# K projections ahead of Q, x of tiles three and four second in SyncE's queue, all MLP weights issued from ScalarE's queue, and new written-out orders, in a one-core transformer block

## The chip, the cores and the metric

The kernel runs on one core of one Trainium2 chip. The metric is the time of one execution on the device in microseconds (us). Three runs of the kernel before took 193.61, 193.75 and 194.16 us: median 193.75 us.

## The reference

What is computed is one transformer block on x of 2048 tokens by 448 channels, in bfloat16: linear attention with 16 heads of 28 channels, then a gated MLP with 1792 hidden channels, each behind a layer norm and with a residual.

```python
def _A_ref(x, wqkv, wo):
    qkv = (x @ wqkv).reshape(B, S, 3, H, Dh) -> 3, B, H, S, Dh
    phi = lambda t: jnp.where(t > 0, t + 1, jnp.exp(t)) + 1e-6
    pq, pk = phi(q), phi(k)
    kv = jnp.einsum("bhsd,bhse->bhde", pk, v)
    z = jnp.einsum("bhsd->bhd", pk)
    num = jnp.einsum("bhqd,bhde->bhqe", pq, kv)
    den = jnp.einsum("bhqd,bhd->bhq", pq, z)[..., None] + 1e-6
    return merge_heads(num / den) @ wo

def _B_ref(x, w_gate, w_up, w_down):
    return (_gelu(x @ w_gate) * (x @ w_up)) @ w_down

h  = x + _A_ref(_layernorm(x), wqkv, wo)
h2 = h + _B_ref(_layernorm(h), w_gate, w_up, w_down)
```

kv and z are sums over all tokens, so no attention output can be formed before the K side of every token is done.

## The kernel before

**Tiles and stages.** The 2048 tokens are 16 tiles of 128. Tensor names are those of the profile; the names in this list are those of the recorded work items, and t is the tile.

1. *Layer norm of x.* bnst1_t and bnag1_t (lines 413 and 414, VectorE) give mean and variance, ln1_t and rstd1_t (lines 420 and 422, ScalarE) the inverse deviation. Tiles 0 to 3 are normalised on VectorE (normD_t, line 435), transposed on TensorE (tr0_t and tr1_t, line 443: two halves), and copied out of PSUM by ScalarE (evxA_t, line 448) and VectorE (evxD_t, line 450). Tiles 4 to 15 are normalised on GpSimd (negm1_t and normP_t, lines 417 and 453) and transposed by a DMA transpose on SyncE's queue (xT_t, line 455).
2. *K side.* k_t is four matmuls of 448 columns (line 469), ek_t its exponential on ScalarE (line 480), ck_t and pk_t two VectorE steps that make phi(k) (lines 481 and 482). The V projection is folded: pt_t multiplies phi(k) by the normalised x itself (line 488; four matmuls for a tile up to tile 9, from tile 10 on split into pt1_t, whose column block also carries z, and pt3_t), summed over all tiles in four PSUM banks.
3. *Q side.* q_t is again four matmuls (line 469), then eq_t and rq_t on ScalarE (lines 496 and 497), and later cq_t, aq_t on VectorE (lines 564 and 565; for pairs p of tiles from the third pair on cqP_p, aqP_p in lines 582 and 583).
4. *The middle.* When the last pt has ended, the sums are copied out (evpD_3 line 516, z1 and z0 lines 514 and 515, evpA_0, evpA_1, evpD_2 lines 519 and 521), multiplied with the V weights (kv, line 527), masked (kvm, line 531), multiplied with the output weights (w2_c, line 547) and copied out again (evwA_c, evwD_c, lines 551 and 553). Two small DMAs (dws0, dws1, line 555) make a copy of these weights with its halves swapped.
5. *Attention output by pairs of tiles (a2_pair).* t1 multiplies by z (line 569 or 585), dr or drP sums (lines 572 and 586), de and rd make 1/den, pn or pnP (lines 576 and 590) normalises. Pair 0 is transposed on TensorE (tro, line 599), pairs 1 to 7 by a DMA transpose on SyncE's queue (oT_p, line 605). The output matmuls are out1_t (line 617) for pair 0 and outA_p, outB_p (lines 627 and 628: two matmuls run at once on the two halves of the rows) for the others. hr_t (line 633) adds the residual, bnst2_t and bnag2_t are the second layer norm's statistics; pair 0 is normalised on VectorE (nhD, wr64, lines 645 and 647) and transposed on TensorE (trh_0, trh_1, line 654; copied out by evhA_0 on ScalarE, line 658, and evhD_1 on VectorE, line 660), the other pairs on GpSimd (negm2, vpe2, pow2, nhP_t, lines 417, 425, 426, 662), copied by VectorE (wrap_t, line 664) and transposed by a DMA on SyncE's queue (hT_t, line 665).
6. *MLP.* In chunks of 2, 2, 4, 4 and 4 tiles. gu2_v or gu4_v (lines 726 and 728) is one unit of gate and up matmuls, which run at once on the two halves of the rows. Unit v writes PSUM bank v % 2 for gate and 6 + v % 2 for up; ge0_v, ge1_v (line 746, ScalarE) apply gelu and hm0_v, hm1_v (line 748, VectorE) multiply into the hidden tensor hh, which frees the banks for unit v + 2. gu2 units 0 to 6 are tiles 0 and 1, 7 to 13 tiles 2 and 3; gu4 units 14 to 27 are tiles 4 to 7, 28 to 41 tiles 8 to 11, 42 to 55 tiles 12 to 15. downA_p and downB_p (line 696) and, for the last two tiles, down448 and down224 (line 678) are the down projection, fo (lines 682, 702) the last residual, do_t (lines 683, 703) the store, on SyncE's queue.

**What sets the order.** Nothing is scheduled at run time. Every work item is recorded with an index; the table ORDERS (lines 15 to 49) has, for each of TensorE, ScalarE, VectorE, GpSimd and SyncE, the indices in the order in which the engine runs them. Semaphore waits are derived from what each item reads and writes. An engine takes its items strictly in order, so an item that waits holds up everything behind it on its engine. HOLD only picks which of several waits is put first. SEQ (line 246) sets the order in which projections are recorded, and with it the indices and which of four PSUM banks each projection gets in turn.

**The loads.** A DMA is issued from SyncE's or ScalarE's queue, in the order of that queue. SyncE's queue has x of tile 0, Wq, x of tiles 2 and 3, Wk, x of tiles 4 to 7, 8 to 11, 12 to 15, the V and output weights, then the twelve xT, then the four gate and up loads, then dws0, dws1, oT_1, oT_2, the down weights, and the later transposes and stores. ScalarE's queue has x of tile 1 and the last 64 rows of Wq and of Wk, then the table load.

The orders of the engines around the places that the prediction's steps touch, in names:

```
TensorE  ... k_12 k_14 pt3_10 k_15 pt1_11 pt1_12 pt1_13 pt3_11 pt3_12 pt1_14 pt1_15 pt3_13 pt3_14 pt3_15 q_4 q_5 kv ...
TensorE  ... out1_0 q_11 out1_1 q_10 q_13 q_15 q_14 outA_1 trh_0 trh_1 q_12 outB_1 gu2_0 gu2_1 outA_2 gu2_2 gu2_3 outB_2 ...
SyncE    ... hT_14 do_3 hT_15 do_4 hT_12 hT_13 ...
```

Of the kernel before, what the change touches and what calls it, by code (L numbers as in the profile page):

```python
# [48 lines left out]
)  # L49
HOLD = {  # L50
    32: (31,), 35: (34,), 66: (36,), 102: (101,), 127: (126,), 166: (165,), 188: (187,), 214: (213,), 294: (292,),
    305: (302,), 323: (302,), 362: (360,), 388: (387,), 498: (378,), 631: (630,), 707: (704,), 745: (744,), 786:
    (672,), 837: (836,), 864: (863,),
}


class _Buf:
# [172 lines left out]
def bass_sequential_preLN__linear_attn_block__glu_gated_geglu__prompt_kernel(  # L230
    nc, A_x, A_wqkv, A_wo, B_x, B_w_gate, B_w_up, B_w_down, out
):
    S, D, FF, H, DH = 2048, 448, 1792, 16, 28
# [14 lines left out]
    G = _Graph()  # L248
    es = ExitStack()
    with es:  # L250
# [8 lines left out]
        wqk_sb = sb("wqk_sb", [128, 4, 2 * D], BF16)  # L259
# [558 lines left out]
```

## Time and profile before

| | us |
|---|---|
| median of three runs | 193.75 |
| the profiled execution, its own time | 193.84 |
| its span (first to last instruction) | 191.9 |
| TensorE busy | 185.7 (97%) |
| VectorE busy | 128.4 (67%) |
| ScalarE busy | 75.2 (39%) |
| GpSimd busy | 50.7 (26%) |

TensorE's busy time is a union of pipelined matmuls, and successive matmuls overlap in it: a group of four matmuls of 448 columns is shown as 0.92 us long, but the next group starts 0.76 us later. So idle time of TensorE is read from starts: the start of one group to the start of the next, less the work of the first.

### The profile page before, as it was taken

Reading aid. Unit: us, or ns where it says so; the run is one execution under the profiler, and the core shown is the slowest. Engines: PE = TensorE matmul, PEld = TensorE weight load, DVE = VectorE, ACT = ScalarE, POOL = GpSimd, SP = SyncE. Lnnn points to the kernel's source line nnn. Section 1 sums busy time; section 2 is a strip of 40 time slices with the busy share of each in tenths; the row PEclk is TensorE's granted clock in tenths of the full one; section 3 lists DMA queues with packets and bytes.
Section 4 is the critical chain, followed back from the end, with each engine's and each line's share of the span. In section 5 each row is a group of like instructions: output and inputs, shape, how many; then the busy total and the mean of one; then the engine's idle time right before and its main releaser. Section 6 shows DMA issues by size and latency. Waiting matters only on the chain.

```text
span 191.9 us, 4456 instructions
## 1 busy us (share of the span) xinstructions
PE 185.7 (97%) x1813; PEld 107.3 (56%) x1813; DVE 128.4 (67%) x328; ACT 75.2 (39%) x220; POOL 50.7 (26%) x91
## 2 busy tenths in 40 slices
PE   7899999999899999999999999999998999999994
PEld 7454445655488677886455445444553445455454
DVE  3799879899799998899993863544723244415223
ACT  3689534699954222335132132432320233411200
POOL 6066730525503478235028000006300000000000
DMA  6985647999295505930221520000193000000025
GB/s 171 377 214 76 106 84 168 222 218 192 55 267 135 96 3 101 149 66 3 48 48 35 108 54 0 0 3 2 35 143 67 3 0 0 27 0 24 3 90 173
DMA packets 35077, 17.11 MB, mean 89 GB/s; under 512 B 26865, under 2 KB 33649, under 8 KB 35057
## 3 DMA queue, kind: packets, MB, share of 16 engines
q1 hardware_dynamic: 34752, 16.60, 40.9%
q8 instruction: 14, 0.23, 0.6%
q10 hardware_dynamic: 304, 0.23, 0.4%
q14 instruction: 7, 0.05, 0.1%
HBM read 8.26 MB, written 1.84 MB: 53 GB/s over the span
## 4 chain that ended last, share of the span: by engine, by line
PE 79%; DVE 11%; DMA 4%; ACT 3%; POOL 0%; SPq 0%; issue 0%
PE ps L728 38%; PE ps L696 19%; PE ps L726 7%; PE ps L469 4%; PE ps L488 3%; PE ps L678 3%; PE ps L627 3%; DMA x_sb<-in_A_x_dram 2%; DVE st L413 2%; PE ps L628 2%; DMA xnT<-xnn 2%; DVE pqn L576 1%; DVE den L572 1%; ACT e L480 1%; DVE x_sb L633 1%; DVE w L553 1%
## 5 line engine op out<-in xcount | busy, mean ns | idle before, releaser
L726 PE MATMUL ps<-hnT,wgu_sb 64*128 64x512 bf16 (+1 forms) x490 | 88.8, 333 | 0.7 <-DVE x_sb L702 0.7
L728 PE MATMUL ps<-hnT,wgu_sb 64*128 64x512 bf16 (+1 forms) x490 | 89.0, 333 | 0.0
L746 ACT ACTIVATE gl<-ps 128x256 bf16<-128x256 f32 x112 | 36.4, 383 | 81.8 <-PE ps L726 78.2
L748 DVE TENSOR_TENSOR hh<-ps,gl 128x256 bf16<-128x256 f32 x112 | 42.4, 416 | 38.6 <-ACT gl L746 38.4
L728 PEld LDWEIGHTS ps<-hnT,wgu_sb 64*128 64x128 bf16 x490 | 44.8, 94 | 31.2 <-DVE hh L748 4.6
L726 PEld LDWEIGHTS ps<-hnT,wgu_sb 64*128 64x128 bf16 x490 | 45.0, 94 | 6.3 <-DMA hnT<-hn 1.2
L696 PE MATMUL ps<-wd_sb,hh 64*128 64x448 bf16 x392 | 41.4, 349 | 0.0
L696 PEld LDWEIGHTS ps<-wd_sb,hh 64*128 64x128 bf16 x392 | 21.8, 94 | 15.8 <-issue 0.4
L469 PE MATMUL ps<-wqk_sb,xnT 128*128 128x448 bf16 x128 | 28.2, 355 | 1.0 <-DMA xnT<-xnn 0.4
L413 DVE BATCH_NORM_STATS2 st<-x_sb 128x6 f32<-128x448 bf16 x32 | 19.3, 615 | 3.2 <-DMA x_sb<-in_A_x_dram 3.1
L469 PEld LDWEIGHTS ps<-wqk_sb,xnT 128*128 128x128 bf16 x128 | 11.9, 98 | 12.7 <-DMA xnT<-xnn 1.3
L585 POOL TENSOR_TENSOR t<-pq,zbc 128x448 f32<-128x448 bf16 x12 | 13.0, 1104 | 19.6 <-DVE pq L583 18.1
L488 PE MATMUL ps<-pk,xnn 128*128 128x448 bf16 x64 | 13.9, 353 | 0.0
L627 PE MATMUL ps<-w,pqnT 64*128 64x448 bf16 x49 | 11.5, 349 | 0.8 <-DVE hn L647 0.8
L702 DVE TENSOR_TENSOR x_sb<-ps,x_sb 128x448 bf16<-128x448 f32 x14 | 8.4, 618 | 5.3 <-PE ps L696 5.3
L480 ACT ACTIVATE e<-ps 128x448 bf16<-128x448 f32 x16 | 8.6, 538 | 5.3 <-PE ps L469 5.1
L417 POOL TENSOR_SCALAR nm<-mv 128x1 f32<-128x1 f32 (+1 forms) x19 | 4.0, 218 | 24.3 <-DVE mv L414 24.0
L662 POOL TENSOR_SCALAR hn<-x_sb,nm,rs 128x448 bf16<-128x448 bf16 x14 | 10.3, 745 | 0.5
L628 PE MATMUL ps<-pt_sb,pqnT 64*128 64x448 bf16 x42 | 10.2, 350 | 0.0
L633 DVE TENSOR_TENSOR x_sb<-ps,x_sb 128x448 bf16<-128x448 f32 x16 | 9.7, 614 | 0.8 <-PE ps L628 0.8
L482 DVE SCALAR_TENSOR_TENSOR pk<-ps,e 128x448 bf16<-128x448 f32 x16 | 9.9, 619 | 0.2
L453 POOL TENSOR_SCALAR xnn<-x_sb,nm,rs 128x448 bf16<-128x448 bf16 x12 | 8.9, 743 | 3.5 <-ACT rs L422 2.9
(83 smaller groups left out, 155.5 us busy)
## 6 DMA issues: line engine op xcount, KB each, us to landing
out_dram<-x_sb SPq DMA_DIRECT2D x15, 112.0 KB, 1.8
wd_sb<-in_B_w_down_dram SPq DMA_DIRECT2D x1, 1568.0 KB, 8.0
x_sb<-in_A_x_dram SPq DMA_DIRECT2D x3, 448.0 KB, 6.3
wgu_sb<-in_B_w_gate_dram SPq DMA_DIRECT2D x1, 896.0 KB, 12.2
wgu_sb<-in_B_w_up_dram SPq DMA_DIRECT2D x1, 896.0 KB, 16.5
wqk_sb<-in_A_wqkv_dram SPq DMA_DIRECT2D x2, 336.0 KB, 4.4
wgu_sb<-in_B_w_gate_dram SPq DMA_DIRECT2D x1, 672.0 KB, 6.1
wgu_sb<-in_B_w_up_dram SPq DMA_DIRECT2D x1, 672.0 KB, 8.6
```

The source lines that it names most:

```text
L413: op("dve", lambda e: e.bn_stats(st[:, t, :], src_ap), [b_src], [b_st[t]], "bnst%s_%d" % (tag, t))
L469: ins = e.matmul(ps[:, bk, 0:D], xnT[:, t, k, :], wqk_sb[:, k, c0:c0 + D], start=(k == 0), stop=(k == 3))
L488: ins = e.matmul(ps[:, BK_PT[c], 0:D], xnn[:, t % XN_R, c * 128:(c + 1) * 128], pk[:, ip, :], start=(t == 0), stop=(t == T - 1))
L585: op("pool", lambda e, n=n: e.tensor_tensor(t1[:, n, :], pq[:, a + n, :], zbc[:, :], ALU.mult), [b_pq[a + n]] + b_z, [b_t1[n]], "t1p_%d" % ...
L627: e.matmul(ps[:, BK_OUT[0], 0:D], pqnT[ra, i2, sg // 2, :], w2[ra, sg // 2, :], start=(sg == 0), stop=(sg == 5))
L628: ins = e.matmul(ps[:, BK_OUT[1], 0:D], pqnT[rb, i2, 3 + (sg + 1) // 2, :], (w2 if sg == 6 else w2s)[rb, sg // 2, :], start=(sg == 0), sto ...
L633: op("dve", lambda e, t=t, bo=bo: e.tensor_tensor(x_sb[:, t, :], ps[:, bo, 0:D], x_sb[:, t, :], ALU.add), [b_ps[bo], b_x[t]], [b_x[t]], "h ...
L696: ins = e.matmul(ps[:, BK_O[n], 0:D], hh[rows, j, sl[n]], wd_sb[rows, j, :], start=(half == 0 and j == 0), stop=(half == 1 and j == NJ - 1))
L726: first = e.matmul(psG[:, jj * N:(jj + 1) * N], wgu_sb[A_, k, j * 128:(j + 1) * 128], hnT[A_, ka_, c0:c0 + N], start=(k == 0), stop=(k == ...
L728: ins = e.matmul(psU[:, jj * N:(jj + 1) * N], wgu_sb[B_, k, j * 128:(j + 1) * 128], hnT[B_, kb_, c0:c0 + N], start=(k == 0), stop=(k == NK ...
L746: G.add("act", lambda e, gi=gi, cs_=cs_, psG=psG: e.activation(gl[:, gi, cs_], psG[:, cs_], AF.Gelu_apprx_tanh), r=[b_ps[BK_G[i]]], w=[b_g ...
L748: op("dve", lambda e, dst=dst, srcU=srcU, srcL=srcL: e.tensor_tensor(dst, srcU, srcL, ALU.mult), [b_ps[BK_U[i]], b_glh], [b_ar[j_][t % HR] ...
```

## The change

The Wk loads take the place of the Wq loads at the head, on ScalarE's queue; x of tiles 2 and 3 moves up to second place in SyncE's queue. The four gate and up loads and the down-weight load move from SyncE's queue to ScalarE's. SEQ starts with K0 K1 in place of Q0, and all five orders are new.

```diff
-    SEQ = "Q0 K0 K1 Q1 K2 Q2 K3 K4 K5 Q3 K6 K7 ...
+    SEQ = "K0 K1 Q0 K2 K3 Q1 K4 Q2 K5 Q3 K6 K7 ...
...
         dma_x("sp", 0, 1)
         dma_x("act", 1, 2)
-        dma_w3("sp", wqk_sb, 0, D, b_wq, "dwq")
-        dma_w1("act", wqk_sb, 0, D, b_wq, "dwq_t")
         dma_x("sp", 2, 4)
-        dma_w3("sp", wqk_sb, D, 2 * D, b_wk, "dwk")
-        tx1 = dma_w1("act", wqk_sb, D, 2 * D, b_wk, "dwk_t")
+        dma_w3("act", wqk_sb, D, 2 * D, b_wk, "dw0")
+        dma_w1("act", wqk_sb, D, 2 * D, b_wk, "dw0_t")
+        tx1 = dma_w1("act", wqk_sb, 0, D, b_wq, "dw1_t")
+        dma_w3("sp", wqk_sb, 0, D, b_wq, "dw1")
...
-            dma("sp", wgu_sb[A_, :, cs], B_w_gate[:, cs]..., "dwg%d" % i, after=xts[-1:])
-            dma("sp", wgu_sb[B_, :, cs], B_w_up[:, cs]..., "dwu%d" % i, after=xts[-1:])
+            dma("act", wgu_sb[A_, :, cs], B_w_gate[:, cs]..., "dwg%d" % i, after=eks[11:12])
+            dma("act", wgu_sb[B_, :, cs], B_w_up[:, cs]..., "dwu%d" % i, after=eks[11:12])
...
-                dma("sp", wd_sb[:, :, :], B_w_down.rearrange("(j p) n -> p j n", p=128), [b_wd], "dwd", after=[G.all[-1]])
+                dma("act", wd_sb[:, :, :], B_w_down.rearrange("(j p) n -> p j n", p=128), [b_wd], "dwd")
```

`after=` only fixes an order on one queue; it is no wait. The two tables of indices say little in themselves. In names, the stretches of the new orders that matter here are:

```
TensorE  warm tr0_0 tr1_0 tr1_1 tr0_1 k_0 k_1 tr0_3 tr1_3 tr0_2 tr1_2 q_0 k_2 k_3 pt4_0 pt4_1 q_1 pt4_2 q_2 k_4 q_3 ...
         ... k_11 q_4 k_12 k_13 k_14 pt4_9 pt3_10 k_15 pt3_11 pt1_10 pt1_11 pt1_12 pt3_12 pt1_13 pt1_14 pt1_15 q_5 pt3_13 pt3_14 pt3_15 q_8 q_6 kv ...
         ... out1_0 out1_1 q_11 q_12 q_13 q_15 q_14 outA_1 trh_0 trh_1 outB_1 gu2_0 gu2_1 outA_2 gu2_2 outB_2 gu2_3 gu2_4 gu2_5 outA_3 gu2_6 outB_3 downA_0 ...
         ... gu4_33 downB_2 gu4_34 gu4_35 gu4_36 gu4_37 downA_3 gu4_38 gu4_39 downB_3 gu4_41 gu4_40 gu4_43 ...
VectorE  wqkpad bnst1_0 bnag1_0 bnst1_1 bnag1_1 normD_0 bnst1_3 normD_1 bnag1_3 evxD_0 bnst1_2 bnag1_2 evxD_1 normD_3 normD_2 ck_0 bnst1_4 ...
         ... pk_14 cq_1 ck_15 pk_15 cq_3 aq_2 aq_3 evpD_3 z0 aq_1 t1d_0 dr_0 evpD_2 ... wr64_0 wr64_1 pnP_2 aqP_3 evhD_1
         hr_2 hr_3 bnst2_2 drP_3 hm0_0 hm1_0 rdP_3 cqP_4 pnP_3 bnag2_2 hm1_1 hm0_1 bnst2_3 bnag2_3 hm0_2 hm1_2 hr_5 hr_4 hm1_3 hm0_3 ...
         ... bnst2_14 fo448_4 hm1_33 hm0_33 bnag2_14 hm1_34 hm0_34 hm0_35 hm1_35 fo448_5 wrap_14 hm1_37 hm1_36 wrap_13 wrap_15 hm0_36 wrap_12 ...
ScalarE  ... ek_13 dwg0 ek_14 dwu0 rq_4 ek_15 dwg1 eq_4 z1 eq_5 rq_5 dwu1 deA_0 evpA_1 evpA_0 ... tbl2 ge0_0 ge1_0 deP_3 dwd ge1_1 ...
SyncE    dx0 dx2 dw1 dx4 dx8 dx12 dwv dwv_t dwo xT_4 xT_5 xT_6 xT_7 xT_8 xT_10 xT_11 xT_9 xT_12 xT_13 xT_14 xT_15 dws0 dws1 oT_1 ...
         ... hT_8 do_3 do_4 do_0 hT_13 hT_15 hT_12 hT_14 do_2 ...
```

The work itself, the number and the shape of every matmul, VectorE, ScalarE and GpSimd instruction and of every transfer, is the same in both.

More of the change, by code (lines that the diff above doesn't have):

```diff
@@ L15 @@
 ORDERS = (
[33 rows of a table removed]
[34 rows of a table added]
 )
 HOLD = {
-    32: (31,), 35: (34,), 66: (36,), 102: (101,), 127: (126,), 166: (165,), 188: (187,), 214: (213,), 294: (292,),
-    305: (302,), 323: (302,), 362: (360,), 388: (387,), 498: (378,), 631: (630,), 707: (704,), 745: (744,), 786:
-    (672,), 837: (836,), 864: (863,),
+    32: (31,), 66: (36,), 99: (98,), 175: (174,), 188: (187,), 232: (231,), 294: (291,), 305: (298,), 362: (360,),
+    388: (387,), 498: (378,), 767: (764,), 787: (786,), 807: (806,), 839: (836,), 864: (863,),
 }
@@ L245, in bass_sequential_preLN__linear_attn_block__glu_gated_geglu__prompt_kernel @@
     T1_DVE = (0,)
-    SEQ = "Q0 K0 K1 Q1 K2 Q2 K3 K4 K5 Q3 K6 K7 K8 K9 K10 K11 K12 K13 Q4 K14 Q5 K15 Q6 Q7 Q8 Q9 Q10 Q11 Q12 Q13 Q14 Q15"
+    SEQ = "K0 K1 Q0 K2 K3 Q1 K4 Q2 K5 Q3 K6 K7 K8 K9 K10 K11 K12 K13 Q4 K14 Q5 K15 Q6 Q7 Q8 Q9 Q10 Q11 Q12 Q13 Q14 Q15"
     G = _Graph()
@@ L509, in bass_sequential_preLN__linear_attn_block__glu_gated_geglu__prompt_kernel @@
             cs = slice(0, FC) if i == 0 else slice(FC, FF)
-            dma("sp", wgu_sb[A_, :, cs], B_w_gate[:, cs].rearrange("(k p) n -> p k n", p=64), [b_wg[i]], "dwg%d" % i, after=xts[-1:])
-            dma("sp", wgu_sb[B_, :, cs], B_w_up[:, cs].rearrange("(k p) n -> p k n", p=64), [b_wu[i]], "dwu%d" % i, after=xts[-1:])
+            dma("act", wgu_sb[A_, :, cs], B_w_gate[:, cs].rearrange("(k p) n -> p k n", p=64), [b_wg[i]], "dwg%d" % i, after=eks[11:12])
+            dma("act", wgu_sb[B_, :, cs], B_w_up[:, cs].rearrange("(k p) n -> p k n", p=64), [b_wu[i]], "dwu%d" % i, after=eks[11:12])
         op("act", lambda e: e.activation(zbc[B_, :], ps[B_, BK_PT[3], 0:D], AF.Identity), [b_ps[BK_PT[3]]], [b_z[1]], "z1")
```

67 rows, old and new, of the table ORDERS are left out of this document.

## The prediction

> **What bounds the kernel now.** I read the page's slices first, then busy time by stretch, then TensorE's starts one by one.
>
> ```profile
> PE   7899999999899999999999999999998999999994
> DVE  3799879899799998899993863544723244415223
> ```
> ```profile
> core 0: us, PE busy (x) PEld busy (x) DVE busy (x) ACT busy (x) POOL busy (x), PEclk, DMA share, GB/s
> 5.30:12.90 7.60, 6.97 (x46) 3.64 (x45) 6.47 (x22) 5.54 (x21) 2.38 (x8) 1.00 0.99 328
> ...
> 35.60:52.10 16.50, 15.69 (x117) 8.64 (x116) 15.31 (x36) 15.57 (x39) 8.54 (x10) 1.00 0.86 164
> 52.10:110.00 57.90, 57.90 (x755) 39.94 (x751) 50.49 (x121) 19.32 (x58) 22.55 (x34) 1.00 0.44 89
> ```
>
> TensorE is full almost everywhere (slices of 4.8 us); VectorE is nearly as full until about 75 us. TensorE's granted clock is 1.00 in all three stretches, so its work is the same in both kernels, and only its idle time can change. I looked for that idle time between starts:
>
> ```profile
> 6.18 0.76 PE L469 MATMUL ps<-wqk_sb,xnT 128*128 128x448 bf16 x2 [0.26 <-ACT xnT L448]
> 7.30 0.55 PE L469 MATMUL ps<-wqk_sb,xnT 128*128 128x448 bf16 x2 [0.37 <-DVE xnT L450]
> ...
> 18.38 0.93 PE L469 MATMUL ps<-wqk_sb,xnT 128*128 128x448 bf16 x4
> ...
> 19.90 0.92 PE L469 MATMUL ps<-wqk_sb,xnT 128*128 128x448 bf16 x4
> 21.23 0.93 PE L469 MATMUL ps<-wqk_sb,xnT 128*128 128x448 bf16 x4 [0.40 <-DMA xnT<-xnn]
> ...
> 45.81 2.43 PE L469 MATMUL ps<-wqk_sb,xnT 128*128 128x448 bf16 x12
> 49.05 0.36 PE L627 MATMUL ps<-w,pqnT 64*128 64x448 bf16 x1 [0.81 <-DVE hn L647]
> ...
> 52.14 0.27 PE L728 MATMUL ps<-hnT,wgu_sb 64*128 64x256 bf16 x1
> ...
> 52.25 0.27 PE L728 MATMUL ps<-hnT,wgu_sb 64*128 64x256 bf16 x1
> ...
> 142.53 3.02 PE L696 MATMUL ps<-wd_sb,hh 64*128 64x448 bf16 x28
> 146.27 0.39 PE L726 MATMUL ps<-hnT,wgu_sb 64*128 64x512 bf16 x1 [0.72 <-DVE x_sb L702]
> ```
>
> From 18.38 to 19.90 stand two groups of four matmuls: 0.76 a group, 0.19 a matmul. So q_0 has 0.74 idle between its halves (7.30 - 6.18 - 0.38), k_7 comes 0.57 late (21.23 - 19.90 - 0.76) behind its x transpose, outA_1 0.96 late (49.05 - 45.81 - 12 x 0.19). A down group of 28 takes 2.65 in this row of the chain, so the first unit of the last chunk at 146.27 is 1.09 late (3.74 - 2.65):
>
> ```profile
> 65.65 2.65 PE ps L696 x28
> ```
>
> Two of these are not what they seem. The one at 146.27 is put down to VectorE, but what it also needs, the last of four DMA transposes, is issued in a row of SyncE's queue that runs from 140.92 to 144.54, and the xT transposes below land 2.4 to 4.3 us after issue. And the wait at 49.05 is nearly free: the MLP cannot start before evhD_1, which VectorE's own queue delivers at 51.53 (50.91 + 0.62).
>
> ```profile
> 32.94 0.62 DVE L482 SCALAR_TENSOR_TENSOR pk<-ps,e 128x448 bf16<-128x448 f32 x1
> 33.48 0.38 DVE L565 TENSOR_TENSOR pq<-pq,eq 128x448 bf16<-128x448 bf16 x1
> 34.13 0.62 DVE L516 CAST pt_sb<-ps 64x448 bf16<-64x448 f32 x1 [0.27 <-PE ps L488]
> ...
> 50.91 0.62 DVE L660 COPY hnT<-ps 128x896 bf16<-128x896 bf16 x1 [0.18 <-PE ps L654]
> ```
> ```profile
> 34.10:51.60 17.50, 16.71 (x39) 1.00 0.89 172
> 52.30:77.60 25.30, 23.06 (x57) 1.00 0.53 125
> ```
>
> From evpD_3 to the end of evhD_1 VectorE runs 39 instructions in 17.40 us and is 95% busy (these two rows: stretch, its length, VectorE busy). Here VectorE, not TensorE, sets the pace.
>
> **The change part by part.** *Start.* Before, evxD_0 stands behind bnst1_2, which waits for x of tiles 2 and 3. Now it stands behind bnst1_3 and normD_1, which TensorE waits for anyway, and k_0 needs only Wk. The 0.74 goes; I expect 0.3 of it back at pt4_1, which now has only four projections and fewer fillers ahead while pk_1 is still in VectorE's queue. Gain 0.4. The bound lies in the landing of x of tiles 2 and 3, third in SyncE's queue:
>
> ```profile
> 6.43 0.63 DVE L413 BATCH_NORM_STATS2 st<-x_sb 128x6 f32<-128x448 bf16 x1 [1.19 <-DMA x_sb<-in_A_x_dram]
> ```
> ```profile
> L346 SPq DMA_DIRECT2D wqk_sb<-in_A_wqkv_dram x1: 419/419/419, 1.2 to 1.2; - x1
> ...
> DMA to landing us min/median/max: 3.7/3.7/3.7
> ```
>
> It lands at 6.4, while VectorE asks at 5.2 (6.43 - 1.19). The second place in the queue, held by 336 KB of Wq, was issued at 1.2 and landed 3.7 later, at 4.9. For 224 KB in that place I take 5.1, when bnst1_3 would ask. If it stays at 6.4, bnst1_3 stalls 1.2 with normD_1 and evxD_0 queued behind it, and the transposes and k_0 wait for those: the gain becomes a loss of 0.5. If all goes well it is 0.9.
>
> The Trainium skill ("DMA: Bandwidth & Descriptors", Queues, rings and completion order) says that each DMA engine takes packets in turn from the queues that have work. By that rule Wk, now on the other queue, takes every second packet, and 224 KB of x cost as much as 448 KB together; at the 328 GB/s of the first stretch above the 112 KB beyond Wq's 336 make 0.3 us more. By it the sum below would be about 0.2 higher; no row here has two large loads on two queues.
>
> *K stage.* The x transposes go in tile order with fewer stalls ahead, and q_1 to q_3 fill TensorE while they land; xT_7 is fourth in SyncE's queue instead of fifth, at 1.3 us each. I take 0.6 of the 0.75 (0.57 and a smaller 0.18 before k_6); bounds 0 and 0.75. One more Q projection stands ahead of k_15, less one pt matmul: 0.57 later. The weight issues on ScalarE cost about 0.65 each:
>
> ```profile
> 28.83 0.67 SPq L346 DMA_DIRECT2D wgu_sb<-in_B_w_gate_dram  x1
> ```
>
> dwg0 and dwu0 stand ahead of ek_14 and ek_15; ScalarE idles there by 0.2 to 0.8 at a time, so I count 0.1 for ek_15, and the whole 0.65 if that cover is gone. So pk_15 moves by 0.57 - 0.4 - 0.6 + 0.1 = -0.33 (bounds -1.1 and +1.7).
>
> *The middle.* Behind pk_15 now stand cq_3, aq_2 and aq_3 (0.2 + 0.3 + 0.3 from start to start) where aq_0 and a wait stood (34.13 - 33.48): evpD_3 comes 0.15 later relative to pk_15. The 39 instructions up to evhD_1 are the same ones, so 17.40 again. q_12 and outB_1 no longer follow evhD_1's input on TensorE, so gu2_0 starts as evhD_1 ends. Together: 51.53 - 0.33 + 0.15 + 0.05 = 51.4 against 52.14. **Gain 0.7**; bounds from the ones above: -1.3 and +1.5. dws0, dws1 and oT_1 no longer queue behind the gate and up loads; whether oT_1 lands at 47 or again at 49, outA_1 and the transposes after it still fit ahead of evhD_1.
>
> *First MLP units.* VectorE's pair work now stands earlier among the products hm. For hm0_1 I add what precedes it from hr_2: six of 0.54 or less (hr, hr, statistics, cqP, rdP, bnag: 2.3), drP 1.0, pnP 1.05, four hm of 0.34: 5.75, against gu2_3 asked for 5.9 after gu2_0 (three units of 14 steps of 0.11, seven steps of 0.19 for outA_2 and outB_2). Durations are start to start: pk_15, 0.62 long, is followed after 0.54 above, and so these rows count 0.07 less each:
>
> ```profile
> L748 DVE TENSOR_TENSOR hh<-ps,gl 128x256 bf16<-128x256 f32 x112 | 42.4, 416 | 38.6 <-ACT gl L746 38.4
> ```
> ```profile
> 46.86 1.05 DVE L586 TENSOR_REDUCE den<-t 128x32 f32<-128x896 f32 x1
> ...
> 49.65 1.08 DVE L590 TENSOR_TENSOR pqn<-pq,rd 128x896 bf16<-128x896 bf16 x1
> ```
>
> The slack is 0.3 there, and again 0.3 to 0.4 at gu2_5 and gu2_6, where the old order had 1.0. Such a sum leaves out short waits, so **I count a loss of 0.3**, bounds 0 and 1.5. The down weights are issued by ScalarE behind deP_3, some 3.4 us later than now, at about 54.5; 8.0 to land gives 62.5, and downA_0 asks at about 65.
>
> ```profile
> wd_sb<-in_B_w_down_dram SPq DMA_DIRECT2D x1, 1568.0 KB, 8.0
> ```
>
> *Last chunk.* Now, two stores stand between the four hT, and the last wrap follows hm0_38.
>
> ```profile
> 137.13 1.22 SPq L665 DMA_TRANSPOSE hnT<-hn  x1
> 138.40 0.58 SPq L703 DMA_DIRECT2D out_dram<-x_sb  x1
> ...
> 140.92 3.62 SPq L665 DMA_TRANSPOSE hnT<-hn  x2
> ```
> ```profile
> 133.86 2.11 POOL L662 TENSOR_SCALAR hn<-x_sb,nm,rs 128x448 bf16<-128x448 bf16 x3
> ```
>
> The four take 7.4 us of SyncE. In the new order the last wrap follows hm0_36, and the stores come before. Counted from the end of downB_2, the second statistics are done after about 1.7, GpSimd's chain of two vpe/pow and four norms (0.7 each by its row) after 7.0, the wraps by 8.6, and four transposes of 1.3 to 2.3 with 3 to land by 15.6 to 16.9; gu4_43 asks at 17.4 (eight units of 1.5, seven steps of 512 columns each, and two down groups of 2.65). So **the 1.09 goes**; bounds 0 and 1.09. Other stretches, and the end, keep what they have.
>
> Sum, against the profiled execution's own 193.84: - 0.7 + 0.3 - 1.1 = 192.3; that execution is 0.09 above the median, so 192.3 after rounding.
>
> **The rivals.**
> *A: the first 52 us give nothing.* x of tiles 2 and 3 lands as late as now, or the transposes still stall k_6 and k_7. For it: the landing rows above and the DMA share of 0.99 in the first stretch. Against it: the new place in the queue. Only the 1.09 stays, less 0.3: 193.0, up to 193.6.
> *B: VectorE's queue decides (slower).* Place: gu2_3 to gu2_13. VectorE took 25.30 for 23.06 of work from 52.3 on; if the new order has the same 10% of waits in the 22.4 us of work up to hm1_8, the products are 2.2 late against 1 us of slack, and the later pair work (pnP_5, pnP_6 also earlier) repeats half of it. Price 1.2 to 2.5, from a lateness of 0.4 at gu2_3 on; with nothing won before 52 us: 193.84 - 1.1 + 2.0 = 194.7. Against it: TensorE had no gap of 0.1 there before.
> *C: the loads on ScalarE's queue meet the last x transposes (slower).* A transpose alone lands in 2.5, oT_1, among the weight loads, in 5.2:
>
> ```profile
> L455 SPq DMA_TRANSPOSE xnT<-xnn x12: 1189/1264/2379, 11.4 to 27.6; - x12
> ...
> DMA to landing us min/median/max: 2.4/2.5/4.3
> ```
> ```profile
> L605 SPq DMA_TRANSPOSE pqnT<-pqn x1: 1542/1542/1542, 43.8 to 43.8; - x1
> ...
> DMA to landing us min/median/max: 5.2/5.2/5.2
> ```
>
> If xT_15 lands 2.7 late, past k_15's turn by 1.7, everything to gu2_0 moves by it: 192.3 + 1.7 to 2.4 = 194.0 to 194.7. It decides only if ek_13 ends before xT_15 is through; I expect ek_13 near 28.5 and xT_15 at 28.5 to 29.3. The Trainium skill (same page, Issuing engines are not separate DMA queues) speaks for this one: DMAs of all issuers run on the same 16 engines and interleave.
>
> **How the numbers follow.** Forecast 0.55 (its own range 191.3 to 193.1), A 0.21, B 0.15, C 0.09. About 0.3% (0.6 us) is what a measurement tells from no change: below 193.17 is faster, above 194.33 slower. Forecast and a third of A are faster: 0.62; the rest of A and the low part of C the same: 0.15; most of B and C slower: 0.23. The range 190.9 to 194.6 holds the forecast with its best bounds and A, and leaves out the upper part of B and C.
>
> **What would show it.** In the changed kernel: k_0's second half at 6.2 to 6.6 and no wait over 0.3 at k_6 and k_7; pk_15 starting near 32.6; evpD_3 to evhD_1 again 17.2 to 17.6; gu2_0 at 51.0 to 51.8; no gap of TensorE over 0.3 from there to 77; and no gap ahead of gu4_43. Wrong it would be by a VectorE wait for x at 5 to 6.5, by gu2 units that wait for L748, or by xT_15 landing after 31.

## The result, and the profile after

| | before | changed |
|---|---|---|
| median of 8 runs of each, same chip | 193.68 (193.35 to 194.16) | 192.66 (192.14 to 193.30) |
| the profiled execution, its own time | 193.84 | 192.45 |
| its span | 191.9 | 190.7 |

Ratio 0.9948, 95% interval 0.9930 to 0.9966: the changed kernel is 1.0 faster, where the prediction said 1.4. The total came near, but several of its terms did not.

Two stretches, up to the first MLP unit (gu2_0) and from there on, in the view of busy time by stretch; the first fence is of the kernel before, the second of the changed one. The columns after the length are the busy times of TensorE, its weight loads, VectorE, ScalarE and GpSimd.

```profile
0.00:52.14 52.14, 49.23 (x316) 27.62 (x317) 44.35 (x120) 36.05 (x101) 23.21 (x48) 1.00 0.77 171
52.14:191.90 139.76, 136.47 (x1500) 79.67 (x1496) 84.08 (x208) 39.16 (x120) 27.53 (x44) 1.00 0.29 59
```
```profile
0.00:51.89 51.89, 49.35 (x315) 27.62 (x316) 44.26 (x121) 36.31 (x100) 22.66 (x48) 1.00 0.79 174
51.89:190.70 138.81, 136.19 (x1498) 86.00 (x1498) 83.46 (x208) 39.65 (x121) 29.62 (x44) 1.00 0.29 58
```

The clock is 1.00 in all four. The first 52 us gave 0.25, the rest 0.95. TensorE's starts (timeline of the changed kernel) say where:

```profile
6.09 0.40 PE L443 MATMUL ps<-ident,xnn 128*128 128x128 bf16 x4 [0.17 <-DVE xnn L435]
6.32 1.77 PE L469 MATMUL ps<-wqk_sb,xnT 128*128 128x448 bf16 x8
...
15.94 0.92 PE L488 MATMUL ps<-pk,xnn 128*128 128x448 bf16 x4
17.04 0.93 PE L469 MATMUL ps<-wqk_sb,xnT 128*128 128x448 bf16 x4 [0.18 <-DMA xnT<-xnn]
...
18.56 0.92 PE L469 MATMUL ps<-wqk_sb,xnT 128*128 128x448 bf16 x4
19.73 0.92 PE L469 MATMUL ps<-wqk_sb,xnT 128*128 128x448 bf16 x4 [0.25 <-DMA xnT<-xnn]
...
44.75 3.76 PE L469 MATMUL ps<-wqk_sb,xnT 128*128 128x448 bf16 x19
49.35 0.36 PE L627 MATMUL ps<-w,pqnT 64*128 64x448 bf16 x1 [0.85 <-DMA pqnT<-pqn]
...
51.89 0.28 PE L726 MATMUL ps<-hnT,wgu_sb 64*128 64x256 bf16 x1
...
62.83 0.36 PE L627 MATMUL ps<-w,pqnT 64*128 64x448 bf16 x1 [0.19 <-DMA pqnT<-pqn]
...
139.54 2.83 PE L696 MATMUL ps<-wd_sb,hh 64*128 64x448 bf16 x27
...
142.19 0.38 PE L726 MATMUL ps<-hnT,wgu_sb 64*128 64x512 bf16 x1
```

By starts, with 0.19 a projection matmul: k_0 and k_1 run through from 6.32, and the 0.74 between the halves of the first projection is gone. k_5 is 0.34 late (17.04 - 15.94 - 0.76) and k_7 0.41 (19.73 - 18.56 - 0.76): together 0.75, as much as k_6 and k_7 lost before, on other tiles. outA_1 is 1.0 late again (49.35 - 44.75 - 19 x 0.19). outA_3 at 62.83 is a new wait, 0.43 by starts (gu2_5 begins at 60.87 and has 1.53 of work). Behind the last down group of the chunk (28 matmuls from 139.54) the next unit follows after 2.65, the length of the group: the 1.09 is gone. 1.09 less 0.43, with 0.13 more at the end, where fewer stores stand ahead of the last one, makes 0.79 of the 0.95; the rest is not assigned to a wait.

The chain of waits of the changed kernel, in order of time (start, length), names two DMA transposes, oT_1 and oT_3; the view of their line has the times from issue to landing of oT_1 to oT_3, the shortest being oT_2's, which had no load ahead of it:

```profile
43.78 5.53 DMA pqnT<-pqn
...
57.05 5.73 DMA pqnT<-pqn
```
```profile
DMA to landing us min/median/max: 2.9/5.5/5.7
```

VectorE's timeline shows what the first of them did to the middle:

```profile
5.11 0.62 DVE L413 BATCH_NORM_STATS2 st<-x_sb 128x6 f32<-128x448 bf16 x1
...
32.73 0.62 DVE L482 SCALAR_TENSOR_TENSOR pk<-ps,e 128x448 bf16<-128x448 f32 x1
...
34.12 0.62 DVE L516 CAST pt_sb<-ps 64x448 bf16<-64x448 f32 x1
...
51.21 0.62 DVE L660 COPY hnT<-ps 128x896 bf16<-128x896 bf16 x1 [0.81 <-PE ps L654]
```

evhD_1 stood 0.81 idle for the transpose trh_1, which TensorE ran behind outA_1, which waited for oT_1. Before, VectorE's idle there was 0.18.

Why oT_1, issued at 43.78, landed at 49.31 is in the DMA views of the stretches 42.4 to 45 and 46.5 to 49.3. q1 is SyncE's queue and q10 ScalarE's; the columns are packets, MB and share of the 16 DMA engines' time, and for the issues count, KB and time to landing.

```profile
q10 hardware_dynamic: 263, 0.54, 104.2%
...
pt_sb<-w SPq DMA_DIRECT2D x2, 168.0 KB, 5.7
pqnT<-pqn SPq DMA_TRANSPOSE x1, 5.5
```
```profile
q1 hardware_dynamic: 1000, 0.37, 97.0%
q10 hardware_dynamic: 3, 0.00, 0.7%
```

dws0, dws1 and oT_1 were issued from 42.37 on, and up to 45 not one packet of their queue moved: nearly all time went to the up weights that ScalarE had issued at about 35. Only when those were through did SyncE's three get the engines. In this stretch the queues did not share, and from 57 to 60, with oT_3 issued behind the down weights, it was the same: 1236 packets of ScalarE's queue, none of SyncE's. At the start of this execution, however, both moved data within one half microsecond (from 2.5 to 3.0, 84 packets of SyncE's and 122 of ScalarE's), so it is shown for these two stretches and not as a rule.

### The profile page after: what moved, and what is told of

Same layout as the page of the kernel before. It is cut to its first block, busy times and chain, and to the rows that moved or that the text cites. A ratio compares the mean times of both kernels' runs of the same rounds, so it can differ in the third digit from the quotient of the medians.

```text
span 190.7 us, 4456 instructions
## 1 busy us (share of the span) xinstructions
PE 185.5 (97%) x1813; PEld 113.6 (60%) x1813; DVE 127.7 (67%) x328; ACT 76.0 (40%) x220; POOL 52.3 (27%) x91
## 4 chain that ended last, share of the span: by engine, by line
PE 79%; DVE 10%; DMA 9%; ACT 1%; issue 0%
PE ps L728 29%; PE ps L696 19%; PE ps L726 13%; DMA pqnT<-pqn 6%; PE ps L469 5%; PE ps L488 4%; DVE st L413 3%; PE ps L627 3%; PE ps L678 3%; DMA xnT<-xnn 2%; PE ps L628 2%; DMA x_sb<-in_A_x_dram 1%; DVE pk L482 1%; DVE pqn L576 1%; DVE mv L414 1%; DVE w L553 1%
## 5 line engine op out<-in xcount | busy, mean ns | idle before, releaser
L696 PEld LDWEIGHTS ps<-wd_sb,hh 64*128 64x128 bf16 x392 | 23.3, 94 | 14.2 <-issue 0.2
L469 PE MATMUL ps<-wqk_sb,xnT 128*128 128x448 bf16 x128 | 26.9, 353 | 0.4 <-DMA xnT<-xnn 0.4
L702 DVE TENSOR_TENSOR x_sb<-ps,x_sb 128x448 bf16<-128x448 f32 x14 | 8.4, 617 | 8.3 <-PE ps L696 8.3
L662 POOL TENSOR_SCALAR hn<-x_sb,nm,rs 128x448 bf16<-128x448 bf16 x14 | 11.0, 792 | 0.3
L488 PEld LDWEIGHTS ps<-pk,xnn 128*128 128x128 bf16 x64 | 6.3, 98 | 5.8 <-DVE pk L482 0.2
```

The lines of the kernel that those rows point to most:

```text
L469: ins = e.matmul(ps[:, bk, 0:D], xnT[:, t, k, :], wqk_sb[:, k, c0:c0 + D], start=(k == 0), stop=(k == 3))
L488: ins = e.matmul(ps[:, BK_PT[c], 0:D], xnn[:, t % XN_R, c * 128:(c + 1) * 128], pk[:, ip, :], start=(t == 0), stop=(t == T - 1))
L696: ins = e.matmul(ps[:, BK_O[n], 0:D], hh[rows, j, sl[n]], wd_sb[rows, j, :], start=(half == 0 and j == 0), stop=(half == 1 and j == NJ - 1))
```

## The experiments

Times are compared through the ratio to the kernel before on the same occasion; the changed kernel's is 0.9948. Line numbers in the kernels below differ by a few from those of the profile above.

**1. The last up load behind oT_1.** The changed kernel with one load moved:

```
-ScalarE ... eq_5 rq_5 dwu1 deA_0 ...     SyncE ... dws0 dws1 oT_1 oT_2 ...
+ScalarE ... eq_5 rq_5 deA_0 ...          SyncE ... dws0 dws1 oT_1 dwu1 oT_2 ...
```

> The changed kernel, with the last of the four gate and up loads (896 KB, the up weights of the hidden units from 768 on) issued by SyncE right behind oT_1 instead of by ScalarE at about 35. Theory (what is issued later waits until the loads issued before it are through, whichever queue they stand in): dws0 and dws1 land by 45.5 instead of 48.0 and 48.6, oT_1 by 47.2 instead of 49.3; the 1.0 that TensorE lost ahead of outA_1 goes, VectorE's 0.81 of idle ahead of evhD_1 goes with it, gu2_0 starts near 51.1 instead of 51.9, and the time falls by 0.8 against the changed kernel, to about 191.9. Rival 1 (VectorE's work up to evhD_1 sets the pace, as the prediction said, and oT_1's lateness is nearly free): outA_1's wait goes and comes back ahead of gu2_0; the time falls by 0.2 at most. Rival 2 (the queues share the DMA engines packet by packet): the load behind oT_1 slows it, oT_1 lands after 48.5, and the time falls by less than 0.3.

Measured: 191.86, ratio 0.9916 (0.9889 to 0.9943). In the profiled execution the stretch 42.3 to 45 of the DMA view has nothing but SyncE's queue, and VectorE's row of evhD_1 has no wait:

```profile
q1 hardware_dynamic: 167, 0.35, 54.7%
...
wgu_sb<-in_B_w_up_dram SPq DMA_DIRECT2D x1, 896.0 KB, 7.3
pt_sb<-w SPq DMA_DIRECT2D x2, 168.0 KB, 2.7
pqnT<-pqn SPq DMA_TRANSPOSE x1, 3.1
```
```profile
50.18 0.62 DVE L662 COPY hnT<-ps 128x896 bf16<-128x896 bf16 x1
```

oT_1 takes 3.1 instead of 5.5 with 896 KB issued right behind it, so a load behind does not slow it and a load ahead does. The queue share of the engines falls to 55% because nothing is left to move at first. evhD_1 comes 1.03 earlier (51.21 to 50.18), of which 0.13 was already there at pk_15. The theory holds; the rivals, that VectorE sets the pace anyway and that queues share, do not. This rests on the trace, in which gu2_0 starts at 50.86 instead of 51.89: by time alone the interval overlaps the changed kernel's (0.9930 to 0.9966).

**2. The same edit in the kernel before.**

```
-SyncE ... dwg0 dwu0 dwg1 dwu1 dws0 dws1 oT_1 oT_2 ...
+SyncE ... dwg0 dwu0 dwg1 dws0 dws1 oT_1 dwu1 oT_2 ...
```

> The kernel before, with the last of its four gate and up loads moved behind oT_1 in SyncE's queue, the same edit that gave the changed kernel 0.8. Theory (in the kernel before oT_1's lateness was nearly free, as the prediction said, because VectorE delivered evhD_1 late anyway: 0.18 of idle ahead of it; in the changed kernel VectorE stood 0.81 idle there): oT_1 lands near 47 instead of 49.0, the 0.97 ahead of outA_1 goes, but gu2_0 moves by 0.2 at most, to 51.9 or later; the time stays within 0.3 of the kernel before. Rival (the wait was as dear before as after): gu2_0 starts near 51.3 and the time falls by 0.8.

Measured: 193.97, ratio 1.0051 (1.0030 to 1.0073). TensorE's timeline:

```profile
48.22 0.36 PE L628 MATMUL ps<-w,pqnT 64*128 64x448 bf16 x1
...
51.37 0.28 PE L727 MATMUL ps<-hnT,wgu_sb 64*128 64x256 bf16 x1
...
55.63 0.36 PE L628 MATMUL ps<-w,pqnT 64*128 64x448 bf16 x1 [1.03 <-DMA pqnT<-pqn]
```

outA_1 comes 0.83 earlier and gu2_0 0.77 earlier (51.37 against 52.14), as the rival had it. So the wait was nearly as dear before as after: in the kernel before, TensorE itself still ran q_12 and outB_1 between outA_1 and gu2_0, and that chain, not evhD_1, ended last. VectorE's part moved by 0.21 only: evhD_1 starts at 50.70 instead of 50.91, and ends at 51.32, just ahead of gu2_0. The 0.77 was lost again at once: oT_2, issued at 50.81 while the moved load was still landing, took 4.8, and outA_2 waited 1.2. Why it took so long here, where the same order of loads in the changed kernel gave oT_2 in 3.3, is not settled. The span is only 0.2 longer (192.1 against 191.9), while the median lies 0.9 above that of the kernel before on this occasion (193.97 against 193.03). The profile of the kernel before is of another occasion, on which it took 193.84, so the two traces can't settle that difference.

**3. The down weights behind oT_2, as before.**

```
-ScalarE ... deP_3 dwd ge1_1 ...     SyncE ... oT_1 oT_2 oT_3 ...
+ScalarE ... deP_3 ge1_1 ...         SyncE ... oT_1 oT_2 dwd oT_3 ...
```

> The changed kernel, with the load of the down weights issued by SyncE behind oT_2 (about 51.2), as in the kernel before, instead of by ScalarE at about 54.6. Theory (oT_3, issued at 57.05, waited for the 1568 KB ahead of it): the load is through by about 59 instead of 61.8, oT_3 lands near 60 instead of 62.8, TensorE's 0.43 ahead of outA_3 goes, and the time falls by 0.4 against the changed kernel, to about 192.25. Rival (outA_3 is late by VectorE's pair work, the issue of oT_3 itself, not by its transfer): oT_3 is issued and lands as now, the time stays within 0.15 of 192.66.

Measured: 192.27, ratio 0.9942 (0.9915 to 0.9969), too near 0.9948 to be told apart by time, so the expected 0.4 is not shown by it. In the trace oT_3 is issued as before, at 57.2, lands 3.6 later, and the view of waits has no row for TensorE from 52 to 80, so outA_3's 0.43 is gone (the span is 190.4 instead of 190.7). The view of oT_3's line:

```profile
L604 SPq DMA_TRANSPOSE pqnT<-pqn x1: 1233/1233/1233, 57.2 to 57.2; - x1
...
DMA to landing us min/median/max: 3.6/3.6/3.6
```

**4. Both together.** Edits 1 and 3 in the changed kernel.

> The changed kernel with two loads moved: the last up load behind oT_1 and the down load behind oT_2, both in SyncE's queue. Theory: the two gains are of different waits and add up (0.8 at outA_1 and gu2_0, 0.45 at outA_3): about 191.4, oT_1 landing near 46.7, oT_3 near 60, no wait of TensorE over 0.25 between 45 and 170. Rival (the two loads, 2.4 MB within 7 us, now stand ahead of oT_2 or oT_3 together): oT_2 or oT_3 lands later than TensorE asks, and the time is that of one edit alone, 191.9 or more.

Measured: 191.29, ratio 0.9904 (0.9880 to 0.9928), span 189.2. Between 45 and 170 us the view of waits has no row for TensorE, and the two stretches are

```profile
0.00:50.89 50.89, 49.14 (x315) 27.87 (x316) 44.26 (x121) 36.33 (x100) 21.64 (x47) 1.00 0.75 174
50.89:189.20 138.31, 135.95 (x1498) 88.99 (x1498) 83.50 (x208) 39.88 (x121) 30.53 (x45) 1.00 0.30 60
```

1.0 less up to gu2_0 and 0.5 less behind it: the two gains add up. That is read from the traces; by time the gain is less sure. The interval lies only just below the changed kernel's (0.9930 to 0.9966), and on this same occasion experiment 5 gave 0.9915 for a kernel that later ran as fast as the changed one.

**5. The four gate and up loads on SyncE's queue again.** The changed kernel, with the four loads behind xT_15; run twice, the second time beside the changed kernel itself.

```
-            dma("act", wgu_sb[A_, :, cs], ..., "dwg%d" % i, after=eks[11:12])
-            dma("act", wgu_sb[B_, :, cs], ..., "dwu%d" % i, after=eks[11:12])
+            dma("sp", wgu_sb[A_, :, cs], ..., "dwg%d" % i, after=xts[-1:])
+            dma("sp", wgu_sb[B_, :, cs], ..., "dwu%d" % i, after=xts[-1:])
```

> The changed kernel, with its four gate and up loads back in SyncE's queue behind xT_15, as in the kernel before (the down weights stay with ScalarE). Theory (what is issued first goes first, whichever queue it stands in): dws0 lands near 48 and oT_1 near 49.3, as with two queues; outA_1 again waits 1.0; the time stays within 0.3 of the changed kernel's 192.66. Rival 1 (the change gained by taking these loads off SyncE's queue): oT_1 lands later than 50, the time rises by 0.5 or more. Rival 2 (the loads on ScalarE cost ScalarE's work behind them): the time falls by 0.3 or more.

> The changed kernel as it is, beside the next run on the same chip, because the two were timed on different occasions so far (ratios to the kernel before of 0.9948 and 0.9915, whose intervals overlap). Both theories: ratio near 0.995.

> The changed kernel with its four gate and up loads in SyncE's queue behind xT_15, once more. Theory (the choice of the queue is worth nothing by itself, since what is issued first goes first): within 0.3 of the changed kernel of the same occasion. Rival (the four issues on ScalarE, which stand between the exponentials of the last K tiles, cost something, or the loads on a queue of their own are served differently): faster than the changed kernel by 0.5 or more.

Measured: first 191.79, ratio 0.9915 (0.9886 to 0.9943), which left it open; then, side by side, 192.09 at 0.9952 (0.9936 to 0.9969) against the changed kernel's 192.05 at 0.9945 (0.9925 to 0.9965). The same. The stretch 42.4 to 45 of the second run shows one queue, as full as two were, and dws0 and oT_1 no later:

```profile
q1 hardware_dynamic: 271, 0.55, 104.8%
...
pt_sb<-w SPq DMA_DIRECT2D x2, 168.0 KB, 4.8
pqnT<-pqn SPq DMA_TRANSPOSE x1, 4.7
```

That part of the change, the gate and up loads on ScalarE's queue, is worth nothing by itself. The first run also shows how far one occasion can stray: it gave 0.9915, as low as experiment 1.

**6. The kernel before, with its two stores out of the way.**

```
-SyncE ... hT_14 do_3 hT_15 do_4 hT_12 hT_13 do_8 ...
+SyncE ... hT_14 hT_15 hT_12 hT_13 do_3 do_4 do_8 ...
```

> The kernel before, with two output stores (tiles 3 and 4) moved behind the last x transpose for the MLP (hT_13) in SyncE's queue; nothing else. Theory (the prediction's last step: SyncE's queue, in which the two stores stand between the transposes, made hT_13 land at 146.2, when gu4_43 could have begun at 145.2): hT_13 lands about 1.2 earlier, the 1.09 ahead of gu4_43 goes, and the time falls by 1.0 to 1.1, from 193.68 to about 192.6. Rival (the wait is for the VectorE additions behind the down groups, as the profile names it): gu4_43 starts as late as before and the time stays within 0.2 of 193.68.

Measured: 192.90, ratio 0.9966 (0.9943 to 0.9989). SyncE's and TensorE's timelines:

```profile
137.47 5.96 SPq L663 DMA_TRANSPOSE hnT<-hn  x4
143.47 1.07 SPq L701 DMA_DIRECT2D out_dram<-x_sb  x2
```
```profile
142.87 2.83 PE L694 MATMUL ps<-wd_sb,hh 64*128 64x448 bf16 x27
...
145.51 0.38 PE L724 MATMUL ps<-hnT,wgu_sb 64*128 64x512 bf16 x1
```

The unit starts 2.64 after the down group, so nothing is left of the 1.09, although VectorE's additions, which the profile had named, were not touched. It was SyncE's queue. The view of waits of the kernel before did name the transposes, in the rows of the weight loads (PEld) that go with the matmuls of outA_1 and of this unit, which start a little earlier than the matmuls:

```profile
PEld ps L627 <- DMA pqnT<-pqn: 1.3, 1, 1.3
...
PEld ps L726 <- DMA hnT<-hn: 1.2, 1, 1.2
```

The time fell by 0.7, with an interval of 0.2 to 1.1 that holds the expected 1.0.

**7. x of tiles 2 and 3 third in SyncE's queue.**

```
-SyncE dx0 dx2 dw1 dx4 ...
+SyncE dx0 dw1 dx2 dx4 ...
```

> The changed kernel with the load of x of tiles 2 and 3 third in SyncE's queue again, behind the 336 KB of Wq, as it stood in the kernel before. Theory (the prediction's bound for the start: bnst1_3 stands ahead of normD_1 and evxD_0 on VectorE, and stalls for x): x lands near 6.2 instead of 4.7, bnst1_3 starts near 6.2 instead of 5.1, k_0's second half near 7.5, and the start loses about 1.0; the time is 0.6 to 1.0 above the changed kernel's 192.66. Rival (Wk now stands on the other queue, so x in third place lands about as early as before in second): bnst1_3 starts by 5.4 and the time stays within 0.3 of 192.66.

Measured: 194.45, ratio 1.0051 (1.0013 to 1.0090). VectorE's timeline:

```profile
6.36 0.63 DVE L412 BATCH_NORM_STATS2 st<-x_sb 128x6 f32<-128x448 bf16 x1 [1.16 <-DMA x_sb<-in_A_x_dram]
```

bnst1_3 waits 1.16 and everything behind it is 1.25 late (6.36 against 5.11; k_0 at 7.57 against 6.32). The second place in the queue is what makes "K first" work at all: without it the changed kernel is slower than the kernel before. The price is more than was expected: by the two ratios it is 2.0 above the changed kernel, against 0.6 to 1.0. The profiled execution took 193.18, among the shorter of its runs; that most took about 1.3 more is not explained by the trace.

**8. More of TensorE's instructions ahead of the K stage.** k_5 and k_7 wait for x transposes, and these stall once in the K stage. The changed kernel with another warm-up:

```
-            for _ in range(WARM):
-                ins = e.matmul(ps[:, 3, 0:128], ones_bf[:], ones_bf[:], start=True, stop=True)
+            for n in 16 * [128] + 48 * [64]:
+                ins = e.matmul(ps[:, 3, 0:n], ones_bf[:], ones_bf[:, 0:n], start=True, stop=True)
```

> The changed kernel, with 64 warm-up matmuls (16 of 128 columns, 48 of 64) instead of 40 of 128: as many columns, 24 more pairs of weight load and matmul. The 16 KB that the trace lists as instruction traffic came at 13.8 and at 43.6, and the DMA engines moved nothing from 15.1 to 16.9 while SyncE's issue of xT_6 took 2.57 instead of 1.27. Theory (it is TensorE's own instruction stream, and DMA transposes stop while it is fetched): with 48 more of TensorE's instructions ahead the first fetch comes some 4.5 us earlier, near 9.3, before any transpose is issued; no xT issue takes over 1.6, xT_5 lands at 15.1 instead of 17.0, the waits at k_5 (0.34) and k_7 (0.41) go, pk_15 starts near 32.0, and the time falls by 0.5 to 0.8, to about 192.0. Rival 1 (the stall belongs to the transposes or to SyncE, whatever TensorE fetches): xT_6's issue again takes 2.5, and the time stays at 192.66. Rival 2 (the thinner warm-up, or the fetch amid the first loads, costs the start what the K stage wins): no stall at k_5 and k_7, but k_0 later than 6.6 and the time within 0.3 of 192.66.

Measured: 194.65, ratio 1.0048 (1.0022 to 1.0074). The stretch 11 to 18 in 40 slices (busy share of the DMA engines in tenths), for the changed kernel, for this one, and for experiment 7:

```profile
DMA  9999984259992006899990000000000899800059
```
```profile
DMA  9999967149999000001599910029993000799600
```
```profile
DMA  9999610000000002999300469999400000003999
```

A slice is 0.175 us. The longest empty piece lies at 14.7 to 16.4, at 13.3 to 14.2, and, where everything was 1.25 late, at 16.1 to 17.3 (the earlier empty piece of that row ends with its first transpose, issued at 12.45). By the trace's DMA records the 16 KB of instruction traffic began at 13.74, 12.11 and 15.01: about 1 us ahead each time. Whose instructions they are is on the changed kernel's page:

```profile
PE 185.5 (97%) x1813; PEld 113.6 (60%) x1813; DVE 127.7 (67%) x328; ACT 76.0 (40%) x220; POOL 52.3 (27%) x91
...
q8 instruction: 14, 0.23, 0.5%
```

14 packets of 16 KB go with 3626 instructions of TensorE (matmuls and weight loads), one for every 259; no other engine has a tenth of that. And the first packet came earlier when TensorE alone got more instructions. In this run the first two transposes were issued at 11.19 and 12.56 as in the changed kernel, so it is not they that moved the stall: it moves with TensorE's instruction stream, as the theory said. But 48 more instructions moved the packet by 1.6 only, not out of the transposes: xT_4 now took 3.8 to land, k_4 waited 0.5, and pt4_7 and pt4_8 0.65, so nothing was won. The median lies 1.6 above the profiled 193.01, and the trace does not say why.

**9. A filler for the wait at k_7.** best_a, and q_4 moved into the wait:

```
-SEQ ... Q3 K6 K7 K8 K9 K10 K11 K12 K13 Q4 K14 Q5 ...
+SEQ ... Q3 K6 K7 Q4 K8 K9 K10 K11 K12 K13 K14 Q5 ...
-TensorE ... k_6 k_7 ... k_11 q_4 k_12 k_13 k_14 pt4_9 pt3_10 k_15 ...
+TensorE ... k_6 q_4 k_7 ... k_11 k_12 pt4_9 k_13 k_14 pt3_10 k_15 ...
-ScalarE ... ek_6 rstd1_9 ek_7 ... ek_8 eq_3 ... ln1_14 rq_3 ... dwu0 rq_4 ek_15 dwg1 eq_4 ...
+ScalarE ... ek_6 rstd1_9 eq_3 rq_3 ek_7 ... ek_8 eq_4 ... ln1_14 rq_4 ... dwu0 ek_15 dwg1 ...
```

> best_a, and in the K stage the projection q_4 (0.76 of TensorE, its x transposed long before) moved from behind k_11 to between k_6 and k_7, with its and q_3's two activations each moved earlier on ScalarE and pt4_9 ahead of k_13. Theory (k_7 waits 0.6 for its x transpose, because the transposes stall for about 2 us at 14 to 17, and q_4 has room there): the wait at k_7 goes, pk_15 starts near 32.0 instead of 32.6 to 32.7, and the time falls by a further 0.4 to 0.65, to about 190.9. Rival 1 (the last transposes set the end of the stage: xT_13 and xT_14 land at 27.6 and 28.1): the wait returns at k_13 or k_14, the time is best_a's. Rival 2 (ScalarE, with two more activations ahead of ek_7 and ek_8, becomes the stage's bound): waits for exponentials at pt4_5 to pt4_8, the time is best_a's or up to 0.5 more.

Measured: 193.30, ratio 1.0009 (0.9988 to 1.0030). TensorE's timeline:

```profile
30.09 0.73 PE L487 MATMUL ps<-pk,xnn 128*128 128x448 bf16 x3
32.31 0.93 PE L468 MATMUL ps<-wqk_sb,xnT 128*128 128x448 bf16 x4 [1.49 <-DVE pk L481]
```

Neither rival: the wait at k_7 went and 1.65 came at k_15 (32.31 - 30.09 - 3 x 0.19), not for a transpose or an exponential but for VectorE. The new sequence gives k_15 the PSUM bank of k_12, and pk_12, which empties it, stood late in VectorE's order.

**10. The same, with pk_12 earlier.**

```
-VectorE ... cq_2 cq_0 ck_13 pk_13 ck_14 ck_12 aq_0 pk_12 pk_14 ...
+VectorE ... cq_2 cq_0 ck_12 pk_12 ck_13 pk_13 ck_14 aq_0 pk_14 ...
```

> best_b, with ck_12 and pk_12 moved ahead of ck_13 on VectorE. In best_b TensorE stood 1.65 ahead of k_15, which takes over the PSUM bank of k_12 in the new sequence and so waited for pk_12, seventh in VectorE's queue behind pk_9 and issued at 31.6. Theory (the filler works and only this wait undid it): pk_12 runs near 29.0, k_15 starts near 30.7, pk_15 near 32.4, the time is 0.1 to 0.4 below best_a, about 191.0. Rival (the last x transposes set the end of the stage, as rival 1 of best_b had it): k_13, k_14 or k_15 waits for its transpose instead, pk_15 at 33 or later, and the time is best_a's or more.

Measured: 191.14, ratio 0.9882 (0.9844 to 0.9920). k_15 follows at once:

```profile
30.29 0.73 PE L487 MATMUL ps<-pk,xnn 128*128 128x448 bf16 x3
30.86 0.92 PE L468 MATMUL ps<-wqk_sb,xnT 128*128 128x448 bf16 x4
```

The cause of the 1.65 is shown. The gain over best_a is not: the intervals overlap, and pk_15 starts at 32.71 against best_a's 32.63, because q_4 (for pk_5) and pt4_9 (for pk_9) now wait 0.25 each and k_5 waited 0.2 in this execution. Both versions beat the kernel before; against the changed kernel (0.9930 to 0.9966) best_c's interval lies below its own, best_a's only just.

## Why the prediction was right, and where it was not

By the two stretches TensorE's idle time is 6.2 before (191.90 - 49.23 - 136.47) and 5.2 after (190.70 - 49.35 - 136.19); that is the 1.0 of the medians.

*Start: right in kind, too small.* 0.75 was gained against a forecast of 0.4: the 0.3 that was to come back at pt4_1 did not. x of tiles 2 and 3 landed at 4.7, sooner than the 5.1 forecast, and bnst1_3 ran at 5.11 without a wait. Experiment 7 shows the condition that the prediction named to be the one that decides, and the price at its bound: 1.25 at k_0, which would turn the 0.75 into a loss of 0.5.

*K stage: wrong.* Of the 0.75 at the x transposes 0.6 was to go; nothing went. The step that failed is the reading of these waits as a matter of the transposes' order and of fillers. They come from one stall of the transposes, next to an instruction fetch (experiment 8): xT_5, issued at 12.56, landed at 16.99, 1.9 later than the 2.5 of an undisturbed one, and all behind it shifted. In the new orders it hit other tiles: 0.34 at k_5 and 0.41 at k_7 here, 0.10 and 0.70 in the changed kernel's second profile (after_same). pk_15 came at 32.73 all the same, against 32.6 forecast, because the better start made up for most of it: 0.57 for one more Q projection, less 0.75, is 0.18 earlier, and 0.21 was measured. The 0.1 for the weight issues on ScalarE is not to be seen: ScalarE stood idle for 0.87 ahead of ek_15, waiting for TensorE.

*Middle: wrong.* gu2_0 was to come 0.7 earlier and came 0.25 earlier. The failed step is the sentence that the wait at outA_1 is nearly free, and that oT_1 might as well land at 49. oT_1 landed at 49.3, evhD_1 stood 0.81 idle behind it, and experiment 1 got the 0.8 back by moving one load. Experiment 2 shows that the reading was wrong of the kernel before too: there TensorE's own chain through q_12 and outB_1 carried the wait to gu2_0. The sum of 17.40 from evpD_3 to evhD_1 hid this. It came out as 17.71 (34.12 to 51.83), but 0.81 of that was waiting; with the wait gone (best_a) it is 16.8 (34.02 to 50.84). The 17.40 held waits too: 0.37 at 38.09, where VectorE waited for ScalarE, and the 0.18 at evhD_1. They were counted as work, and the first is gone in the new order.

*First MLP units: right size, wrong cause.* The 0.3 was to be lost to VectorE's order at gu2_3, gu2_5 and gu2_6. None of these units waited. 0.43 was lost at outA_3, where the prediction had looked only at downA_0: the down weights landed at 61.8, as forecast (62.5), early enough for downA_0, but oT_3 stood behind them.

*Last chunk: right.* The 1.09 went, as forecast, and experiment 6 shows by two stores alone that it was SyncE's queue and not VectorE.

*The rivals.* A, that the first 52 us give nothing, came nearest: they gave 0.25. The measured 192.66 lies midway between the forecast's 192.3 and A's 193.0. That the total still fell within the forecast's own range is in part luck: the last chunk's term carried it, and the better start covered for the K stage. B did not happen. C happened to other transposes than the ones named: ek_13 ended after xT_15 had been issued, so the last x transposes were clear of the loads, but oT_1 and oT_3 were not. That the loads stood on ScalarE's queue did nothing for or against oT_1 (experiment 5); for oT_3 no run tells the queue of the down load from its time of issue. At the start the prediction weighed a rule of the Trainium skill ("DMA: Bandwidth & Descriptors", Queues, rings and completion order): each DMA engine takes packets in turn from the queues that have work. The rows of 42.4 to 45 don't agree: one queue had 104% of the engines and the other, with three transfers issued, no packet. Nor did the 0.3 that it would have added at the start appear, where x came 0.4 sooner than forecast without it. What the same page of the Trainium skill states under Issuing engines are not separate DMA queues, that DMAs of all issuers run on the same 16 engines, agrees with experiment 5 (104.8% with one queue, 104.2% with two); that they interleave does not agree with the rows of 42.4 to 45.

## What to carry to other kernels

A small DMA that TensorE waits for should be issued ahead of a bulk load, not beside it: another queue did not protect it here, and moving two loads behind two transposes brought, by ratios of different occasions, nearly as much as the whole change (0.9948 to 0.9904). Look then at the next small DMA, too: in the kernel before, the load moved behind oT_1 was still landing when oT_2 was issued, and the 0.77 was lost again (experiment 2). Where a wait of TensorE is put down to an engine, read the row of its weight loads as well. Before a wait is called free, follow what stands behind it on its own engine to the next common point, and test the sum of a stretch for idle time inside it: a stretch that keeps its length can be one that waits. Moving one projection also moves PSUM banks, so the engine that empties the bank must move with it.

## What the runs showed of the hardware that was not expected

Two queues with work did not alternate in the middle of this kernel: from 42.4 to 45 the queue with the older loads had the DMA engines to itself. With one queue in place of two, dws0 and dws1 took 4.8 instead of 5.7 and oT_1 4.7 instead of 5.5, issued 0.55 later: they landed within 0.4 of the same time.

TensorE's instruction stream comes over the same DMA engines, 16 KB for about every 259 instructions, and DMA transposes in flight at that time landed 1.3 to 1.9 late: in the three executions above an empty piece of 0.9 to 1.8 follows the start of the fetch by about 1. In the K stage, where transposes run almost without a break from 11 to 28, the fetch always met them. The hT transposes of the MLP show both cases. In the changed kernel an instruction packet (of TensorE's queue q8, or of q14, whose engine is not known) began while five of the 14 were in flight, and these took 4.3 to 5.1 to land; the other nine took 3.0 to 3.2. In the kernel before it is again five and nine, 3.7 to 4.6 against 2.9 to 3.1. That the fetch causes the stall rests on this and on the shifts of experiment 8; no run took the fetch away from the transposes of the K stage.
